# Three priorities, one planner bound and one store's queue at the end of a gated attention and state-space kernel

## The chip, the cores and the metric

The kernel runs on one core of one Trainium2 chip. The metric is the device time of one execution in microseconds (us), as the median of several runs. A profiled execution of its own gives the trace. Its span runs from the first to the last instruction, and its device time is somewhat longer than its span.

## The reference, cut to what matters

The output is a gated mix of two branches over the same sequence length of 2048 and width of 448, in bfloat16: `g * a + (1 - g) * b`, where `g` is a sigmoid per row.

```
q = (x @ wq), 16 heads of 28;  k = x @ wk;  v = x @ wv        # one key and value head for all
p = softmax(q k^T * 28 ** -0.5);   a = (p v, heads side by side) @ wo
K = Re(sum over 256 modes of C * exp(dt * A * l) * dt * B)    # 448 channels, l = 0..2047
b = causal convolution of u with K (length 2048) + u * Dskip
g = sigmoid(sum(x * gate_w));   out = g * a + (1 - g) * b
```

Both branches take the same x: the reference passes x as u.

## The kernel before, in words

The two branches are interleaved on one core.

**Attention.** There are 16 passes of 64 tiles: a pass is one group of four heads over 512 query rows, a tile is 128 keys by 512 queries. `qk` (inside `main`, L1280 and L1289) makes the scores on TensorE, ScalarE exponentiates two or three tiles at once (L1313), and `pv` (L1331) multiplies by the values and by a column of ones, which gives the softmax denominators. The last pass is walked in another order (function `dec`): queries 0 to 255, then 256 to 383, then 384 to 511, so that the first query rows are done earlier. `norm_last` then normalizes such a piece: the sums leave PSUM by a VectorE copy (`evac`, L1186), an fp32 product by a 0/1 matrix spreads the denominators over the partitions (L1201), VectorE takes the reciprocal (L1204) and multiplies (L1205).

**Output.** `outp(qc, tt)` multiplies 128 normalized rows by `Wo` in four accumulating products, g = 0 to 3 (L1155; for the very last 128 rows the same four are written out in `tail`, L1222), and `fold` (L1164) adds g times the result into the output tile `O` on VectorE. Below, "3.0" to "3.3" are the four 128-row pieces of the last 512 queries; "3.1 g3" is the fourth product of piece 3.1.

**Convolution.** For each of 28 groups of 16 channels, `conv(c)` multiplies Toeplitz blocks, which are loaded from a DRAM scratch, by the inputs (L1112), gates and flips the sum (L1127), turns it back with four small products (L1138), and adds it into `O` on VectorE (L1146). The groups 26 and 27 own the last 32 columns of `O`, which have dependence keys `Oz` of their own.

**Stores.** `tail` writes the output by DMAs. `out0` to `out3` carry the first 416 columns, four row blocks each (three for `out3`), from SyncE. `outz0` and `outz1` carry the last 32 columns in pieces of 64 bytes: `outz0` the first half of the row blocks, from GpSimd; `outz1` the rest but the last block, from ScalarE's queue. `outl0` and `outl1` carry the last row block (3.3), halves on SyncE and ScalarE. Each is one or two DMA instructions. A queue issues in order, and SyncE waits for all of them at the end.

**What sets the order.** Nothing is written by hand: `Prog.schedule` is a list scheduler that runs at build time with a planned duration for each operation. On each engine it takes, among the operations that are ready at the same planned time, the one with the lower `pr`; operations with `pr` of 2 or more also get some planned slack (`SLACK`). The result is one fixed instruction list per engine with semaphore waits. A PSUM bank is taken by the first operation with `lock` and given back by the one with `unlock`. `Prog.idle` (called for each TensorE operation) puts *zero products* into planned gaps of TensorE: products with three zero columns of `vaug`, which add nothing (L1346). It does so only while `FILL[0] < r < FILL[1]` in planned time, while the planned load of the last 3413 ns is under `LOW`, and while `self.part < 15`. That counter is set at every `pv`:

```
            t = 4 * v + 3
            pg.parts[len(pg.ops) - 1] = v % 16 if t < HF - 64 else 15
```

`HF - 64` is 896 of 1024 tiles, so from tile 896 on the counter stays at 15.

Of the kernel before, what the change touches and what calls it, by code (L numbers as in the profile page):

```python
# [66 lines left out]
def dram(t, off, dims):  # L67
    return bass.AP(tensor=t.tensor, offset=t.offset + off, ap=[list(d) for d in dims])
# [7 lines left out]
class Prog:  # L76
# [8 lines left out]
    HEAD = 0.4  # L85
    RANK = {142: -3000, 102: -1500, 107: 1500, 188: -700, 28: -1500, 23: -3000, 121: -3000, 33: 1500, 57: 1500, 93: -700, 181: -700}
    POOL = (7, 5)
    LOW, SPAN, FILL = .47, 3413.0, (36000.0, 440000.0)
    AHEAD = 1500.0
    SLACK = {"pe": 700.0, "dve": 150.0}  # L90

# [331 lines left out]
def el(n, rate=0.96, fix=68):  # L423
    return fix + n / rate
# [22 lines left out]
class Kernel:  # L447
# [647 lines left out]
    def conv(self, c):  # L1095
        pg = self.pg
        X = ("cx", c)
        cs = c % 2
        ps = px = self.grp()
        tls = []  # L1100
        for k in range(4):
            tls.append(self.tload(4 * c + k))
            if k == 0:
                ps.conv = [self.lastT, None]
                pg.convs.append(ps)
        for k in range(4):
            gi = 4 * c + k
            for n in range(8):
                def mm(e, k=k, n=n, tl=tls[k], gi=gi):
                    tbuf, to = pg.hinfo[tl.home]  # L1110
                    for j in range(4):
                        r = e.matmul(ps.v(32 * j, 32 - 2 * n, 128 * k, [[1, 128]]),  # L1112
                                     self.U.v(0, P, (4 * gi + j) * 32 + 2 * n, [[1, 32 - 2 * n]]),
                                     tbuf.v(0, P, to + j * 1024 + 896 - 128 * n, [[1, 128]]),
                                     start=(n == 0), stop=(n == 7), tile_position=(0, 32 * j), skip_group_check=True)
                    return r
                first = k == 0 and n == 0
                ps.conv[1] = len(pg.ops)
                o = pg.op("pe", mm, 56, mode="c", ni=8, rd=[("TL", gi), ("Uc", c)] + ([("U", q) for q in range(4)] if c == 0 else []),
                      wr=[X] + ([("cst", cs)] if first else []), pr=(1.6, 1.0)[c > 25],  # L1120
                      lock=ps if first else None)
                if n == 7:
                    o.tfree = tls[k]
        self.cdone[c] = o.i
        if c % 8 == 7 and c < 24:
            pg.homes.append([[self.cdone[k] for k in range(c - 7, c + 1)], NTR + c // 8])
        pg.op("dve", lambda e: e.tensor_tensor(self.cst.v(0, P, cs * 512, [[128, 4], [64, 2], [1, 64]]),  # L1127
                                               ps.v(0, P, 63, [[128, 4], [64, 2], [-1, 64]]),
                                               self.omq.v(0, P, 0, [[0, 4], [64, 2], [1, 64]]), ALU.mult),
              el(512), rd=[X, "omq"], wr=[("cst", cs), X], pr=2)  # L1130
        Y = ("yx", c)

        def yt(e, k):
            for par in range(2):
                for mu in (0, 1):
                    nt = 15 if (mu == 1 and par == 0) else 16
                    ro = 16 * (1 - par) + mu
                    r = e.matmul(px.v(64 * par, 64, 64 * k, [[16, 4], [1, nt]]),  # L1138
                                 self.cst.v(0, P, cs * 512 + 128 * k + 64 * (1 - mu), [[1, 64]]),
                                 self.ident.v(0, P, ro, [[32, 4], [1, nt]]),  # L1140
                                 start=(mu == 0), stop=(mu == 1), tile_position=(0, 64 * par), skip_group_check=True)
            return r
        for k in range(4):
            pg.op("pe", lambda e, k=k: yt(e, k), 70, mode="h", ni=8, rd=[("cst", cs), "id"], wr=[Y], pr=1.55)
        ov = self.O.v(0, P, 15 * D + 16 * c, [[-D, 16], [1, 16]])
        pg.op("dve", lambda e: e.tensor_tensor(ov, ov, px.v(0, P, 0, [[1, 16], [16, 16]]), ALU.add),  # L1146
              el(256), rd=[Y], comm=tuple(("O" if c < 26 else "Oz", q) for q in range(7)), pr=2, unlock=px)

    def outp(self, qc, tt):
        pg = self.pg  # L1150
        X = ("ox", qc, tt)
        G = self.grp()
        px = lambda: G.v(0, P, 0, [[1, D]])
        for g in range(4):
            pg.op("pe", lambda e, g=g: e.matmul(  # L1155
                px(), self.onT.v(0, P, g * 512 + 128 * tt, [[1, 128]]), self.Wo.v(0, P, g * D, [[1, D]]),
                start=(g == 0), stop=(g == 3), tile_position=(0, 0), skip_group_check=True), 200,
                rd=["Wo"] + [("on", gg) for gg in (0, 1, 2, 4 if (qc, tt) == (3, 2) else 3)], wr=[X], pr=1.2 if qc == 3 else 1.65, lock=G if g == 0 else None)
        self.fold(qc, tt, px, 0, D, [X], unlock=G)

    def fold(self, qc, tt, px, off, n, rd, unlock=None):
# [45 lines left out]
    def tail(self):  # L1207
        pg = self.pg
        self.norm_last(14, 0, 512, None, [("on", 2)])
        self.norm_last(15, 0, 256, None, [("on", 3)])  # L1210
        for tt in range(2):
            self.outp(3, tt)
        self.norm_last(15, 256, 128, None, [("on", 4)])
        self.outp(3, 2)
        self.evac(15, 384, 128)
        self.norm_last(15, 384, 128, 1, [("on", 5)])
        t, o = self.bank(2)
        px = lambda: t.v(0, P, o, [[1, D]])
        X, key = ("ox", 3, 3), [("b", 2)]
        on = [("on", 0), ("on", 1), ("on", 2), ("on", 5)]  # L1220
        for g in range(4):
            pg.op("pe", lambda e, g=g: e.matmul(  # L1222
                px(), self.onT.v(0, P, g * 512 + 384, [[1, 128]]), self.Wo.v(0, P, g * D, [[1, D]]),
                start=(g == 0), stop=(g == 3), tile_position=(0, 0), skip_group_check=True), 200,
                rd=["Wo", on[g]], wr=[X] + key, pr=1 if g < 3 else 0.5)
        self.fold(3, 3, px, 0, D, [X])
        D0 = D - 32
        n0 = len(pg.ops)
        rows = lambda t0, m, d0, n: [(dram(self.out, (1024 * h + 64 * t0) * D + d0, [[D, 64], [64 * D, m], [1, n]]),
                                      self.O.v(64 * h, 64, D * t0 + d0, [[D, m], [1, n]])) for h in range(2)]  # L1230
        for qc in range(4):
            m = 4 if qc < 3 else 3
            pg.dma(rows(4 * qc, m, 0, D0),
                   (128 * m, 832), f"out{qc}", rd=[("O", q) for q in ([qc], range(3, 6))[qc == 3]], pr=1)
        for i in range(n0, len(pg.ops)):
            pg.after[i] = self.lastT
        for k, e in enumerate(("pool", "act")):
            m = 8 - k
            pg.dma(rows(8 * k, m, D0, 32),
                   (128 * m, 64), f"outz{k}", rd=[("Oz", q) for q in (range(2), range(2, 6))[k]], pr=1, eng=e)  # L1240
        for h, e in enumerate(("sp", "act")):
            pg.dma(rows(15, 1, 0, D)[h:h + 1], (64, 896), f"outl{h}", rd=[("O", 6), ("Oz", 6)], pr=1, eng=e)
# [184 lines left out]
```

## Time and profile before

| what | value |
|---|---|
| runs of the kernel | 507.58, 508.55 and 510.98 us, median 508.55 us |
| profiled execution, device time | 510.69 us |
| its span | 508.7 us |
| mean granted TensorE clock | 0.975 of full speed |
| busy ScalarE, VectorE, TensorE | 486.1, 451.2, 433.7 us |
| last exponential ends | about 500.7 us of the span |
| last VectorE instruction ends | about 505.2 us |

How to read it: the attention's exponentials keep ScalarE busy nearly throughout. They are over at about 500.7 us, and what follows is a tail of 8 us with little work, in which the last rows are normalized, multiplied by `Wo`, added up and stored. All times below are microseconds from the start of the span. In a row of the timeline the first number is the start, the second the length, then come engine, line, operation, and the number of merged instructions; square brackets hold the idle time before it and what ended it. "SPq" and "ACTq" are the DMA-issuing instructions of SyncE's and ScalarE's queues; those of GpSimd stand under POOL.

### The profile page before, as it was taken

Reading aid. Unit: us, or ns where it says so; the run is one execution under the profiler, and the core shown is the slowest. Engines: PE = TensorE matmul, PEld = TensorE weight load, DVE = VectorE, ACT = ScalarE, POOL = GpSimd, SP = SyncE. Lnnn points to the kernel's source line nnn. Section 1 sums busy time; section 2 is a strip of 40 time slices with the busy share of each in tenths; the row PEclk is TensorE's granted clock in tenths of the full one; section 3 lists DMA queues with packets and bytes.
Section 4 is the critical chain, followed back from the end, with each engine's and each line's share of the span. In section 5 each row is a group of like instructions: output and inputs, shape, how many; then the busy total and the mean of one; then the engine's idle time right before and its main releaser. Section 6 shows DMA issues by size and latency. Waiting matters only on the chain.

```text
span 508.7 us, 18842 instructions
## 1 busy us (share of the span) xinstructions
PE 433.7 (85%) x8380; PEld 201.5 (40%) x8487; DVE 451.2 (89%) x825; ACT 486.1 (96%) x438; POOL 164.3 (32%) x304
## 2 busy tenths in 40 slices
PE   7888877887878898888888898988888898899795
PEld 5522232433424344433444443343344343443473
DVE  7999999999999999999999999999999998222264
ACT  5999999999999999999999999999999997999893
POOL 8800225412422421442251324225233325050101
PEclk9959999999999999999999999999999997999979
DMA  7988406999597996999999899997979999999902
GB/s 206 234 66 117 99 23 199 279 335 305 183 339 273 345 313 221 303 306 366 312 339 372 251 321 334 339 367 232 379 234 349 339 323 363 368 339 386 353 27 46
DMA packets 115730, 138.45 MB, mean 272 GB/s; under 512 B 48841, under 2 KB 55402, under 8 KB 115650
## 3 DMA queue, kind: packets, MB, share of 16 engines
q1 hardware_dynamic: 105872, 127.82, 79.1%
q0 software_dynamic: 8768, 9.31, 6.9%
q8 instruction: 66, 1.08, 0.9%
q10 hardware_dynamic: 1010, 0.12, 0.1%
q14 instruction: 14, 0.11, 0.1%
HBM read 125.41 MB, written 5.22 MB: 257 GB/s over the span
## 4 chain that ended last, share of the span: by engine, by line
DVE 54%; ACT 29%; PE 14%; issue 2%; DMA 1%; SPq 1%
ACT expT L1313 27%; DVE tab L1005 8%; DVE tab L1016 5%; DVE tab L1017 5%; DVE tab L1027 4%; DVE tab L1015 4%; DVE tab L1014 4%; DVE msq L948 3%; PE psS L1289 3%; DVE tmp L1023 3%; PE psB L1331 2%; PE psS L1280 2%; DVE seedz L952 2%; DVE seedz L950 2%; DVE mbf L968 2%
## 5 line engine op out<-in xcount | busy, mean ns | idle before, releaser
L1313 ACT ACTIVATE expT<-psS 128x1536 bf16<-128x1536 f32 (+1 forms) x410 | 467.1, 1326 | 8.9 <-PE psS L1280 4.7
L1289 PE MATMUL psS<-qM,kT 128*128 128x512 bf16 (+2 forms) x372 | 105.6, 360 | 29.8 <-ACT expT L1313 18.4
L1331 PE MATMUL psB<-expT,vaug 128*32 128x512 bf16 (+2 forms) x1152 | 105.2, 373 | 1.8 <-issue 0.7
L1280 PE MATMUL psS<-qT,kT 29*128 29x512 bf16 (+2 forms) x693 | 83.7, 369 | 26.9 <-ACT expT L1313 23.2
L145 POOL DMA_DIRECT2D KP_scratch<-kstg x112 | 61.4, 556 | 60.0 <-DVE kstg L1067 45.1
L1005 DVE TENSOR_TENSOR tab<-tab,mbf 128x512 bf16<-128x512 bf16 (+3 forms) x56 | 64.5, 1152 | 0.1
L1331 PEld LDWEIGHTS psB<-expT,vaug 128*32 128x32 bf16 x1152 | 28.0, 94 | 78.6 <-issue 73.4
L1289 PEld LDWEIGHTS psS<-qM,kT 128*128 128x128 bf16 x473 | 31.2, 99 | 49.5 <-ACT expT L1313 33.1
L1280 PEld LDWEIGHTS psS<-qT,kT 29*128 29x128 bf16 x693 | 21.8, 93 | 68.5 <-ACT expT L1313 52.9
L145 POOL DMA_DIRECT2D rdenB<-R_scratch x56 | 28.9, 523 | 60.7 <-DMA R_scratch<-denT 41.1
L145 POOL DMA_DIRECT2D qM<-qT x64 | 32.0, 508 | 31.4 <-DVE qT L923 16.9
L1016 DVE TENSOR_TENSOR tab<-tab 128x128 bf16<-128x128 bf16 (+4 forms) x70 | 41.7, 595 | 0.1
L1017 DVE TENSOR_TENSOR tab<-tab 128x128 bf16<-128x128 bf16 (+4 forms) x70 | 41.5, 593 | 0.0
L145 POOL DMA_DIRECT2D denT<-acc x14 | 10.6, 758 | 82.5 <-DVE acc L1186 69.1
L1112 PE MATMUL psX<-T,U 128*32 128x128 bf16 (+3 forms) x1472 | 36.6, 223 | 0.3 <-DVE O L1164 0.3
L1112 PE MATMUL psS<-T,U 128*32 128x128 bf16 (+7 forms) x1248 | 31.1, 222 | 1.5 <-issue 1.1
L1027 DVE TENSOR_TENSOR tab<-tab,tmp 128x4096 bf16<-128x4096 bf16 x14 | 31.9, 2282 | 0.1
L1014 DVE TENSOR_TENSOR tab<-tab,mbf 128x4096 bf16<-128x4096 bf16 x14 | 31.9, 2280 | 0.0
L1015 DVE TENSOR_TENSOR tab<-tab,mbf 128x4096 bf16<-128x4096 bf16 x14 | 31.9, 2280 | 0.0
L1112 PEld LDWEIGHTS psX<-T,U 128*32 128x32 bf16 (+3 forms) x1472 | 25.0, 94 | 16.7 <-issue 12.3
L1052 PE MATMUL psX<-tab 128*32 128x64 bf16 x1152 | 27.2, 242 | 1.8 <-issue 1.4
L145 POOL DMA_DIRECT2D R_scratch<-denT x14 | 8.4, 599 | 62.9 <-DVE denT L1178 35.2
(166 smaller groups left out, 551.8 us busy)
## 6 DMA issues: line engine op xcount, KB each, us to landing
T<-KP_scratch SPq DMA_DIRECT2D x170, 512.0 KB, 8.4
U<-KP_scratch SPq DMA_DIRECT2D x40, 512.0 KB, 9.6
tab<-KP_scratch SPq DMA_DIRECT2D x14, 512.0 KB, 8.2
rdenB<-R_scratch POOLq DMA_DIRECT2D x56, 64.0 KB, 5.5
qM<-qT POOLq DMA_DIRECT2D x64, 32.0 KB, 5.1
tab<-in_A_x_dram SPq DMA_DIRECT2D x8, 224.0 KB, 3.5
O<-cst SPq DMA_DIRECT2D x1, 1792.0 KB, 9.3
KP_scratch<-kstg POOLq DMA_DIRECT2D x112, 16.0 KB, 4.5
```

The lines of the kernel that those rows point to most:

```text
L145: return [e.dma_start(o, i, **kw) for o, i in pairs]
L1005: vo(lambda e, dst=dst, src=src, mri=mri: e.tensor_tensor(dst, src, mri, ALU.mult), 4 * n, done + mk(lv), [kr, ki, tk])
L1014: vo(lambda e, src=src, mi=mi, tv=tv: e.tensor_tensor(tv, src, mi, ALU.mult), 2 * n, done + mk(lv), [tk])
L1015: vo(lambda e, dst=dst, src=src, mr=mr: e.tensor_tensor(dst, src, mr, ALU.mult), 2 * n, done + mk(lv), [kr, ki, ("gap", s)])
L1016: vo(lambda e, dc=dc, tc=tc: e.tensor_tensor(dc[0], dc[0], tc[1], ALU.subtract), n, [tk, kr], [kr])
L1017: vo(lambda e, dc=dc, tc=tc: e.tensor_tensor(dc[1], dc[1], tc[0], ALU.add), n, [tk, ki], [ki])
L1027: vo(lambda e: e.tensor_tensor(tab.v(0, P, FM, [[4, 1024], [1, 4]]), tab.v(0, P, lo + 124, [[CG, 32], [-4, 32], [1, 4]]), rho.v(0, P, 0, [ ...
L1112: r = e.matmul(ps.v(32 * j, 32 - 2 * n, 128 * k, [[1, 128]]), self.U.v(0, P, (4 * gi + j) * 32 + 2 * n, [[1, 32 - 2 * n]]), tbuf.v(0, P, t ...
L1280: r = e.matmul(self.psS.v(0, P, 512 * b + o, [[1, n]]), kT.v(32 * h, DH + 1, 128 * kt, [[1, 128]]), qT.v(32 * h, DH + 1, 512 * (i % 2) + q ...
L1289: r = e.matmul(self.psS.v(0, P, 512 * b + o, [[1, n]]), kT.v(0, P, 128 * kt, [[1, 128]]), self.qM.v(0, P, (i % 2) * XQ + 512 * h + qo, [[1 ...
L1313: pg.op("act", lambda e: e.activation(expT.v(0, P, 512 * es[0], spread(es, n)), self.psS.v(0, P, 512 * bs[0], spread(bs, n)), AF.Exp, scal ...
L1331: r = e.matmul(self.psB.v(32 * h, 32, qo, [[1, n]]), vaug.v(0, P, 32 * kt, [[1, 32]]), expT.v(0, P, 512 * ring[t] + o, [[1, n]]), start=(k ...
```

## The change

Four edits in three functions and one planner constant:

- `FILL`: zero products are allowed until 490 us of planned time instead of 440 us.
- `conv`: the VectorE add of the convolution groups 26 and 27 into `O` gets `pr` 1.5 instead of 2 (and so loses the planned slack).
- `outp`: the output products of the last 512 queries get `pr` 0.9 instead of 1.2, which is below the 1 and 0.5 of `tail`'s own products in the first case and above in the second.
- `tail`: the store `outz0` is issued by SyncE instead of GpSimd.

```
-    LOW, SPAN, FILL = .47, 3413.0, (36000.0, 440000.0)
+    LOW, SPAN, FILL = .47, 3413.0, (36000.0, 490000.0)
...
-              el(256), rd=[Y], comm=tuple(("O" if c < 26 else "Oz", q) for q in range(7)), pr=2, unlock=px)
+              el(256), rd=[Y], comm=tuple(("O" if c < 26 else "Oz", q) for q in range(7)), pr=(2, 1.5)[c > 25], unlock=px)
...
-                ... wr=[X], pr=1.2 if qc == 3 else 1.65, lock=G if g == 0 else None)
+                ... wr=[X], pr=0.9 if qc == 3 else 1.65, lock=G if g == 0 else None)
...
-        for k, e in enumerate(("pool", "act")):
+        for k, e in enumerate(("sp", "act")):
             m = 8 - k
             pg.dma(rows(8 * k, m, D0, 32),
                    (128 * m, 64), f"outz{k}", rd=[("Oz", q) for q in (range(2), range(2, 6))[k]], pr=1, eng=e)
```

What the scheduler makes of it, read from the two built programs: the lists of all five engines, waits included, are the same up to the last 30 or so instructions of TensorE. The 13 zero products stand where they stood and none is added. From there the lists differ as follows (in order; each name is one instruction unless counted):

```
TensorE before  3.1 g0 g1 g2 | 3.3 g0 g1 | last pv x16 | 3.3 g2 | 3.1 g3 | 3.2 g0 | L1201 | 3.2 g1 g2 g3 | 3.3 g3
TensorE after   3.1 g0 g1 g2 g3 | 3.2 g0 | last pv x16 | 3.2 g1 g2 g3 | 3.3 g0 | L1201 | 3.3 g1 g2 | 3.3 g3
VectorE before  fold 3.0 | evac L1186 | fold 3.1 | L1204 | fold 3.2 | L1205 | fold 3.3
VectorE after   fold 3.0 | fold 3.1 | evac L1186 | fold 3.2 | L1204 | L1205 | fold 3.3
GpSimd before   ... outz0 x2                     GpSimd after   ... (ends before it)
SyncE before    out0 out1 out2 (x6) | out3 x2 | outl0
SyncE after     out0 out1 out2 (x6) | outz0 x2 | out3 x2 | outl0
```

ScalarE's list is unchanged: exponentials, then `outz1` x2, then `outl1`.

More of the change, by code (lines that the diff above doesn't have):

```diff
@@ L1157, in outp @@
                 start=(g == 0), stop=(g == 3), tile_position=(0, 0), skip_group_check=True), 200,
-                rd=["Wo"] + [("on", gg) for gg in (0, 1, 2, 4 if (qc, tt) == (3, 2) else 3)], wr=[X], pr=1.2 if qc == 3 else 1.65, lock=G if g == 0 else None)
+                rd=["Wo"] + [("on", gg) for gg in (0, 1, 2, 4 if (qc, tt) == (3, 2) else 3)], wr=[X], pr=0.9 if qc == 3 else 1.65, lock=G if g == 0 else None)
         self.fold(qc, tt, px, 0, D, [X], unlock=G)
```

## The prediction

> **What bounds the kernel now.** I read the page first (shares, the chain that ended last), then the timeline of the last 10 us engine by engine, then the DMA issues and the DMA traffic of the end.
>
> ```profile
> span 508.7 us, 18842 instructions
> PE 433.7 (85%) x8380; PEld 201.5 (40%) x8487; DVE 451.2 (89%) x825; ACT 486.1 (96%) x438; POOL 164.3 (32%) x304
> ...
> L1346 PE MATMUL psB<-vaug,ident x12: 378/390/391, 59.5 to 387.9; 128*128 128x512 bf16 x12
> ```
>
> ScalarE is busy for 486.1 of 508.7 us. But the built lists differ only in the last 30 or so instructions, so the question is what bounds the last 9 us. The chain of waits, restricted to that stretch, says it:
>
> ```profile
> 501.29 0.30 PE psS L1222
> 501.59 0.20 PE psS L1155
> ...
> 501.82 0.69 DVE O L1164
> 502.50 0.86 DVE rdenB L1204
> 503.37 0.50 DVE O L1164
> 503.87 0.21 DVE onT L1205
> ...
> 504.12 0.38 PE psS L1222
> ...
> 504.52 0.68 DVE O L1164
> ```
>
> After the last `pv` VectorE is the chain: fold 3.1, reciprocal, fold 3.2, multiplication, then one product and fold 3.3. Two folds stand in line between the last attention sums and the last product, though they do not belong to it. After that come the stores. The timeline (engines together, rows chosen) has the starts that I count with:
>
> ```profile
> 496.38 0.95 DVE L1204 RECIPROCAL rdenB<-psX 128x128 f32<-128x128 f32 x1
> ...
> 497.36 0.29 DVE L1205 TENSOR_TENSOR onT<-acc,rdenB 128x128 bf16<-128x128 f32 x1
> ...
> 497.75 0.42 DVE L1146 TENSOR_TENSOR O<-O,psS 128x256 bf16<-128x256 bf16 x1
> ...
> 498.46 1.44 POOL L145 DMA_DIRECT2D out_dram<-O  x2 [24.33 <-DVE O L1146]
> ...
> 500.41 0.54 PE L1222 MATMUL psS<-Wo,onT 128*128 128x448 bf16 x2
> ...
> 500.88 0.41 PE L1331 MATMUL psB<-expT,vaug 128*32 128x128 bf16 x16
> ...
> 501.23 0.36 PE L1222 MATMUL psS<-Wo,onT 128*128 128x448 bf16 x1
> ...
> 501.35 0.29 DVE L1186 COPY acc<-psB 128x128 f32<-128x128 f32 x1 [1.28 <-PE psB L1331]
> 501.42 0.54 PE L1155 MATMUL psS<-Wo,onT 128*128 128x448 bf16 x2
> ...
> 501.80 0.38 PE L1201 MATMUL psS<-acc,msq 128*128 128x128 f32 x2
> ...
> 502.42 0.95 DVE L1204 RECIPROCAL rdenB<-psS 128x128 f32<-128x128 f32 x1
> 503.28 0.59 DVE L1164 SCALAR_TENSOR_TENSOR O<-psS,gt,O 128x448 bf16<-128x448 f32 x1
> 503.78 0.28 DVE L1205 TENSOR_TENSOR onT<-acc,rdenB 128x128 bf16<-128x128 f32 x1
> ```
>
> From these rows: products of 448 columns start 0.19 apart (501.23, 501.42). A fold starts 0.40 after the start of its last product (501.42 to 501.82; 504.12 to 504.52) and lets the next VectorE instruction start 0.60 later (501.82 to 502.42). A multiplication starts 0.34 before the product that uses it (503.78 to 504.12).
>
> **The change part by part.**
>
> *Zero products until 490.* Costs and gains nothing. The row of L1346 has the last one at 387.9, so the old bound of 440 was not what stopped them: from tile 896 of 1024 the counter `part` is 15 and forbids them. The built list has the same 13 in the same places (12 of them have a record in the trace). Would they come, each would cost about 0.39 of TensorE.
>
> *The convolution add's priority.* Nothing by itself: both adds keep their place in VectorE's list. The last is at 497.75, ahead of fold 3.0, in both.
>
> *`outz0` from SyncE.* GpSimd loses two issues (1.44 in all, at 498.46), and nothing stands behind them there. SyncE gains a wait for the add that ends at 498.17 and two issues. Queued behind that wait are `out3` and `outl0`. The queue rows of the end, one narrow window each:
>
> ```profile
> 503.90 0.72 ACTq L145 DMA_DIRECT2D out_dram<-O  x1
> 503.90 1.99 SPq L145 DMA_DIRECT2D out_dram<-O  x3
> 505.23 0.65 SPq L145 DMA_DIRECT2D out_dram<-O  x1
> 505.51 0.95 ACTq L145 DMA_DIRECT2D out_dram<-O  x1
> ```
>
> SyncE issues nothing between its first six stores and 503.90. A pair of 64-byte stores takes ScalarE's queue from 503.90 to 505.51, 1.61. On SyncE the pair would run from 498.2 to 499.8, and `out3` will not be wanted before 502.7 (below): hidden by 2.9, cost 0. Its landing:
>
> ```profile
> T<-KP_scratch SPq DMA_DIRECT2D x1, 512.0 KB, 13.6
> out_dram<-O SPq DMA_DIRECT2D x2, 156.0 KB, 2.8
> ...
> out_dram<-O POOLq DMA_DIRECT2D x2, 32.0 KB, 2.2
> out_dram<-O ACTq DMA_DIRECT2D x2, 28.0 KB, 3.2
> out_dram<-O SPq DMA_DIRECT2D x1, 56.0 KB, 2.8
> out_dram<-O ACTq DMA_DIRECT2D x1, 56.0 KB, 2.7
> ```
>
> Bounds are 2.2 (the same store from GpSimd) and 13.6 (a load on SyncE's queue amid full traffic). I take 3.2, the same 64-byte shape on ScalarE's queue: the second lands at about 499.0 + 3.2 = 502.2, long before the end. At 13.6 it would land at 512.6 and set the end; that is a rival.
>
> *The output products' priority.* This is the edit that moves something. TensorE, in the new order, with the pace of 0.19 and the last `pv` left at 500.88 (it waits for ScalarE, and five products stand ahead of it as before):
>
> - 3.1 g3 takes the place at 500.41, and 3.2 g0 that at 500.60. Fold 3.1 starts at 500.81 instead of 501.82, when VectorE is idle, and frees it at 501.41.
> - The copy L1186 now stands behind fold 3.1: 501.41 instead of 501.35, a cost of 0.06. What waits for the copy is L1201.
> - After `pv`: 3.2 g1, g2, g3 at 501.23, 501.42, 501.61, 3.3 g0 at 501.80, L1201 at 501.99 instead of 501.80, because four products stand ahead of it instead of three. Its operand is ready at about 501.75. Done at 502.37.
> - Fold 3.2 starts at 501.61 + 0.40 = 502.01, ends at 502.70, frees VectorE at 502.61. Before it started at 503.28, after the reciprocal.
> - The reciprocal starts at 502.61 instead of 502.42, a loss of 0.19. But no fold follows it. The earlier 128-column reciprocal started 0.98 before its multiplication (496.38 to 497.36). So L1205 starts at 503.59 instead of 503.78, the last product at 503.93, fold 3.3 at 504.33, and its end comes at 505.01 instead of 505.20: 0.19 gained.
> - The stores. `out3` and `outz1` wait for fold 3.2 and can go at 502.73 instead of 503.90, 1.17 earlier. That matters on ScalarE's queue: before, `outl1` was ready at 505.2 but stood behind the pair of `outz1` until 505.51. Now the pair is through at 502.73 + 1.61 = 504.34, so `outl1` goes with the data, at 505.04, 0.47 earlier. `outl0` goes at 505.04 instead of 505.23.
>
> *The last landing.* Before: 505.51 + 2.7 = 508.2 for `outl1`, 505.23 + 2.8 = 508.0 for `outl0`; the span ends 0.5 after the later. With unchanged landings the later is now `outl0` at 507.84: 0.37 gained. The other end: both last stores share the DMA engines with `out3` and `outz1`, which now start 1.17 earlier. The windows of the end show that all traffic is one block of 2.4:
>
> ```profile
> 502.00:505.00 3.00, 1.12 (x6) 0.31 (x4) 2.54 (x5) 0.00 (x0) 0.00 (x0) 1.00 0.00 0
> 505.00:508.70 3.70, 0.00 (x0) 0.00 (x0) 0.21 (x1) 0.00 (x0) 0.00 (x0) 0.76 0.58 133
> ...
> 506.90:507.50 0.60, 0.00 (x0) 0.00 (x0) 0.00 (x0) 0.00 (x0) 0.00 (x0) 0.52 0.99 218
> 507.50:508.10 0.60, 0.00 (x0) 0.00 (x0) 0.00 (x0) 0.00 (x0) 0.00 (x0) 0.50 0.09 28
> ```
>
> (The last two columns are the DMA share and GB/s.) If the block splits, the last stores may land like the only output store of the end that ran alone, GpSimd's 2.2: 507.24, a gain of 0.97. I take the middle, 0.65, since the other stores still overlap part of the last ones. Below nothing the landing has no reason to go, as less is in flight.
>
> [...]
>
> *Sum.* 508.7 - 0.65 = 508.05 of span. The profiled execution took 510.69, 1.99 more than its span, so it would take 510.04. But it is a slow one, 2.14 above the median of the runs (508.55); the median should come to 508.55 - 0.65 = 507.9.
>
> **The rivals.**
>
> - *Nothing gained: the tail is hidden.* If the last landing is set by the whole block of traffic or by a completion that does not depend on its issue, the end stays: 508.5. For it: the DMA share is 0.99 just before the end. Against it: the block's first half starts 1.17 earlier, and 504.0 to 505.1 was free.
> - *Slower: the reciprocal is pushed back.* In the new list two folds stand ahead of the reciprocal. Gain and loss balance where fold 3.2 starts at 502.20 instead of 502.01, since the reciprocal would then start at 502.80 and the multiplication at the old 503.78. If each of the four products takes 0.1 more than I count, or 3.1 g3 does not get out before the last `pv` (then fold 3.1 starts at 501.23 + 0.40, frees VectorE at 502.23, and all behind it is 0.82 behind my list), the last fold ends at up to 505.83 instead of 505.20. `outl0` then goes at 505.86 and lands at 508.66 instead of `outl1` at 508.21: 0.45 slower, a median of 509.0.
> - *Slower: SyncE's small store lands late.* Mechanism: 64-byte pieces on SyncE's ring, landing after the last store. It decides from a landing of about 8.6 (the forecast's last landing at 508.2 - 0.65 = 507.55, less 499.0), and at the bound of 13.6 the last landing is at 512.6 instead of 508.2, 4.4 later: a median of 512.95. Against it: 3.2 on ScalarE's queue, and a DMA share of 0.13 from 498 to 502:
>
> ```profile
> 498.00:502.00 4.00, 4.00 (x77) 2.18 (x76) 1.32 (x4) 2.70 (x3) 1.44 (x2) 1.00 0.13 18
> ```
>
> - *The change does not do what it says.* True for the first edit, as said, and for the second. If the moved products bring nothing either, this is the first rival.
>
> **How the numbers follow.** Forecast (gain 0.37 to 1.04): 0.75. Nothing gained: 0.12. Reciprocal pushed back: 0.11. Late landing: 0.02. The likeliest gives 507.9. The forecast's own bounds are 507.5 to 508.2; the pushed-back case adds 509.0. The runs before lie 0.97 below and 2.43 above their median, and that spread is wider than any term here, so I take about 0.5 beyond the cases at either side: 506.9 to 509.5. One per cent, 5.1 us, is about what a measurement of this kernel can tell from no change, and every case but an extreme landing stays far inside it: within 1% 0.97, faster 0.01, slower 0.02.
>
> **What would show it right or wrong.** Right: fold 3.1 at about 500.8 and ahead of the copy; fold 3.2 about 0.4 to 0.6 before the reciprocal; no fold between reciprocal and multiplication; `out3` and `outz1` issued about 1.2 earlier; `outl1` issued with `outl0`; no traffic left over at their issue; 13 zero products, the last near 388; the pair of `outz0` on SyncE near 498.2. Wrong: a copy later than 501.6, a reciprocal later than 502.8, `outl1` still behind `outz1`, or an `outz0` landing near the end. A difference of more than 2 us anywhere before 499 would mean that something moved which the lists do not show.

## The result and the profile after

The changed kernel takes 507.46 us in the median (505.21 to 509.80, 20 runs); the kernel before, run beside it, 509.27 us (507.19 to 511.44, 20 runs). The ratio is 0.9964, with a 95% interval from 0.9947 to 0.9981. That is 1.8 us less, or 1.0 to 2.7 us by the interval: the same within 1%, as forecast, and faster by more than the 0.65 us forecast.

The profiled execution after took 507.12 us with a span of 505.1 us, against 508.7 before. Most of these 3.6 us are not the change. The last `pv` group started at 500.88 before and starts at 498.32 now, and up to a few products ahead of it the instruction lists are the same, but for the small store that SyncE now issues; below, two executions of one and the same list differ by 4.8 us. So I measure the tail, from the start of the last `pv` group to the end of the span. The rows of that stretch (start, end and length, the busy times of the engines, and last the granted clock, the DMA share and GB/s), before and after:

```profile
500.88:508.69 7.81, 2.24 (x26) 1.06 (x25) 3.22 (x6) 0.00 (x0) 0.00 (x0) 0.89 0.28 63
```

```profile
498.32:505.14 6.82, 2.24 (x26) 1.14 (x25) 3.33 (x6) 0.00 (x0) 0.00 (x0) 0.84 0.33 72
```

The tail takes 7.81 before and 6.82 after: the change is worth 0.99 there. (The expectations below count with spans printed to 0.1, and so with 7.82 and 6.78.) The four edits are two priorities, one bound and one queue; the title counts one priority too many.

The timeline of the changed kernel's tail, the rows that answer to those of the prediction:

```profile
497.27 1.12 PE L1155 MATMUL psS<-Wo,onT 128*128 128x448 bf16 x5
498.24 0.69 DVE L1164 SCALAR_TENSOR_TENSOR O<-psS,gt,O 128x448 bf16<-128x448 f32 x1 [0.74 <-PE psS L1155]
...
498.32 0.41 PE L1331 MATMUL psB<-expT,vaug 128*32 128x128 bf16 x16
...
498.84 0.28 DVE L1186 COPY acc<-psB 128x128 f32<-128x128 f32 x1
...
499.43 0.38 PE L1201 MATMUL psS<-acc,msq 128*128 128x128 f32 x2
499.44 0.68 DVE L1164 SCALAR_TENSOR_TENSOR O<-psS,gt,O 128x448 bf16<-128x448 f32 x1 [0.32 <-PE psS L1155]
...
500.04 0.95 DVE L1204 RECIPROCAL rdenB<-psS 128x128 f32<-128x128 f32 x1
...
501.03 0.29 DVE L1205 TENSOR_TENSOR onT<-acc,rdenB 128x128 bf16<-128x128 f32 x1
...
501.37 0.36 PE L1222 MATMUL psS<-Wo,onT 128*128 128x448 bf16 x1 [1.18 <-DVE onT L1205]
501.78 0.68 DVE L1164 SCALAR_TENSOR_TENSOR O<-psS,gt,O 128x448 bf16<-128x448 f32 x1 [0.46 <-PE psS L1222]
```

What to see: fold 3.1 (498.24) now starts ahead of the last `pv` group, in VectorE's old gap; fold 3.2 (499.44) stands ahead of the reciprocal, and between reciprocal (500.04) and multiplication (501.03) there is no fold. Counted from the last `pv` group, fold 3.3 ends at 4.14 instead of 4.32.

The queues of the changed kernel, one narrow window each, and then its DMA issues with the KB of each and the us to landing:

```profile
495.63 1.27 SPq L145 DMA_DIRECT2D out_dram<-O  x2
...
500.16 2.85 ACTq L145 DMA_DIRECT2D out_dram<-O  x3
...
502.49 0.50 SPq L145 DMA_DIRECT2D out_dram<-O  x1
502.49 0.52 ACTq L145 DMA_DIRECT2D out_dram<-O  x1
```

```profile
out_dram<-O SPq DMA_DIRECT2D x2, 156.0 KB, 2.7
...
out_dram<-O SPq DMA_DIRECT2D x2, 32.0 KB, 2.6
out_dram<-O ACTq DMA_DIRECT2D x2, 28.0 KB, 3.1
out_dram<-O SPq DMA_DIRECT2D x1, 56.0 KB, 1.9
out_dram<-O ACTq DMA_DIRECT2D x1, 56.0 KB, 2.2
```

`outz1` starts at 500.16, 2.33 ahead of the last stores (before, 1.33 ahead of `outl0` and 1.61 ahead of `outl1`), and `outl0` and `outl1` go together at 502.49, with their data. They land in 1.9 and 2.2 instead of 2.8 and 2.7. The 0.99 is made up of 0.18 (end of fold 3.3), 0.28 (`outl1` no longer behind `outz1`: it was issued at 505.51 where `outl0` went at 505.23), and some 0.5 (landing of `outl1`, 2.7 to 2.2, which are known to 0.1).

Why they land earlier is in the DMA engines' busy share. Each digit is that share in tenths (9 is 90% or more) in a slice of 0.12 us; both rows end with the span. Before (from 503.88), then after (from 500.32):

```profile
DMA  0000000000289999874459999889995000000000
```

```profile
DMA  0000000006989988744799999902697930000000
```

Before, the traffic is one block up to 507.6: the last stores' data come right behind those of `out3` and `outz1`. After, the others are still at work when the last stores are issued at 502.49, but they are through at about 503.5; then there is a gap, and the last stores' data follow alone.

### The profile page after: what moved, and what is told of

Same layout as the page of the kernel before. It is cut to its first block, busy times and chain, and to the rows that moved or that the text cites. A ratio compares the mean times of both kernels' runs of the same rounds, so it can differ in the third digit from the quotient of the medians.

```text
span 505.1 us, 18842 instructions
## 1 busy us (share of the span) xinstructions
PE 432.4 (86%) x8380; PEld 200.1 (40%) x8487; DVE 451.7 (89%) x825; ACT 486.3 (96%) x438; POOL 162.9 (32%) x302
## 4 chain that ended last, share of the span: by engine, by line
ACT 44%; DVE 35%; PE 16%; issue 3%; DMA 1%; SPq 1%
ACT expT L1313 43%; DVE tab L1005 5%; PE psS L1289 3%; DVE tab L1016 3%; DVE tab L1017 3%; PE psB L1331 3%; PE psS L1280 3%; DVE tab L1027 3%; DVE tab L1015 3%; DVE tab L1014 3%; DVE msq L948 2%; PE psS L1112 2%; DVE tmp L1023 2%; DVE seedz L952 1%; DVE mbf L968 1%
```

## The experiments

Each ratio is to the kernel before, run beside it on the same chip. The medians themselves are from several chips (the kernel before had 508.41 beside e1 to e4, 508.12 beside e5 to e8 and 509.39 beside e9 to e12), so only the ratios can be compared. "Tail" is the time from the start of the last `pv` group to the end of the span in that kernel's one profile; where the number of runs is 1, the profiled execution is all there is.

| kernel | median us (runs) | ratio to before, 95% interval | last pv, span | tail us |
|---|---|---|---|---|
| before | 509.27 (20) | 1 | 500.88, 508.69 | 7.81 |
| changed | 507.46 (20) | 0.9964, 0.9947 to 0.9981 | 498.32, 505.14 | 6.82 |
| e1 order only | 506.82 (12) | 0.9965, 0.9941 to 0.9988 | 497.31, 504.15 | 6.84 |
| e2 store only | 507.62 (12) | 0.9972, 0.9947 to 0.9997 | 498.99, 506.81 | 7.82 |
| e3 same lists as before | 508.90 (12) | 1.0005, 0.9982 to 1.0027 | 496.35, 504.16 | 7.81 |
| e4 changed, again | 507.20 (12) | 0.9974, 0.9950 to 0.9999 | 500.01, 506.83 | 6.82 |
| e5 before, outz1 from GpSimd | 518.1 (1) | | 503.16, 515.92 | 12.77 |
| e6 changed, early stores delayed | 508.16 (12) | 0.9994, 0.9971 to 1.0016 | 497.47, 504.29 | 6.82 |
| e7 changed, fold 3.2 behind | 506.35 (1) | | 496.44, 504.28 | 7.84 |
| e8 before, early stores delayed | 509.94 (12) | 1.0027, 0.9998 to 1.0055 | 500.14, 508.03 | 7.89 |
| e9 order only, GpSimd's store later | 513.42 (1) | | 502.68, 511.42 | 8.74 |
| e10 changed, out3 with full rows | 508.02 (12) | 0.9972, 0.9952 to 0.9991 | 497.13, 503.96 | 6.83 |
| e11 store only, again | 507.96 (12) | 0.9988, 0.9965 to 1.0011 | 498.05, 505.88 | 7.83 |
| e12 same lists, again | 510.05 (12) | 1.0025, 1.0001 to 1.0049 | 501.17, 509.03 | 7.86 |

The theories: A, the new order of the output products is all of the gain, and it lies in the tail; B, the store's move to SyncE gains too. C and D (a stall near 479) and E (GpSimd's closing drain) came up on the way.

**e1: the order alone.** Of the four edits only this one:

```
-                ... wr=[X], pr=1.2 if qc == 3 else 1.65, ...
+                ... wr=[X], pr=0.9 if qc == 3 else 1.65, ...
```

> Only the output products' priority (0.9), the store stays on GpSimd. Theory A (the order of the tail is all of it): from the start of the last pv group to the end of the span 6.8 us as in the changed kernel (7.82 before, 6.78 after), fold 3.2 about 0.6 before the reciprocal, outl1 issued with outl0; time about 1.0 us under the kernel before. Theory B (the store's move to SyncE brings the rest of the 1.8): the tail is at most 0.3 shorter than before, or the time is 0.8 us longer than that of the changed kernel.

Measured: a tail of 6.84 and a ratio of 0.9965. Fold 3.2 starts 0.60 ahead of the reciprocal, and `outl1` is issued with `outl0`, as expected. For the tail theory A holds to within 0.02. The time fell by 1.8, where A expected 1.0.

**e2 and e11: the store alone.**

```
-        for k, e in enumerate(("pool", "act")):
+        for k, e in enumerate(("sp", "act")):
```

> Only outz0 from SyncE instead of GpSimd, order of the products as before. Theory A: tail from the last pv group to the end 7.8 us, time equal to the kernel before within 0.7 us; the pair is issued when the last convolution add is done and lands within 3.5 us. Theory B: the time falls by about 0.8 us.

> outz0 from SyncE alone, once more. Theory A (no effect but through the closing drain, which the old order hides): time of the kernel before within 0.7 us, tail 7.8. Rival (something ahead of the tail gets faster): 1.4 us under the kernel before again, as the first time.

Measured: tails of 7.82 and 7.83, so nothing in the tail. The times were 0.9972 the first time, outside of what theory A allowed, and 0.9988 the second, inside it. The traces show no place where such a gain would arise.

**e3 and e12: the two edits that change no list.**

```
-    LOW, SPAN, FILL = .47, 3413.0, (36000.0, 440000.0)
+    LOW, SPAN, FILL = .47, 3413.0, (36000.0, 490000.0)
...
-              ... for q in range(7)), pr=2, unlock=px)
+              ... for q in range(7)), pr=(2, 1.5)[c > 25], unlock=px)
```

> Only the later bound for zero products and the convolution add's priority: the built instruction lists are those of the kernel before. Theory A: ratio 1.000, tail 7.8 us, 13 zero products, the last near 388; what the medians of this run differ by from the kernel before is the size of the scatter. Rival (the scatter is a property of the build): a ratio clearly off 1, by 0.8 us or more.

> The instruction lists of the kernel before, once more, as the yardstick for the store-only kernel on the same chip: ratio 1.000 within 0.0015, tail 7.8.

Measured: tails of 7.81 and 7.86, and the zero products where they were, the last at 388.7 in e12:

```profile
L1346 PE MATMUL psB<-vaug,ident x13: 379/389/390, 59.6 to 388.7; 128*128 128x512 bf16 x13
```

The times are what matters here: with the instruction lists of the kernel before, the ratio came out at 1.0005 and at 1.0025, the second outside the 0.0015 expected and with an interval that leaves 1 out. So a ratio of this kernel is uncertain by some 0.0025, 1.3 us, more than its own interval says. The spans of the two profiles differ by 4.8 us.

**e4: the changed kernel once more.** No edit.

> The changed kernel once more. Theory A: tail 6.8 us again, and a time about 1.0 us under the kernel before, so 0.998 of it, nearer to that than to the 0.9964 measured. Rival (something before the tail became faster too): 0.9964 again, 1.8 us, with the start of the last pv group earlier than in the kernels with the old order.

Measured: tail 6.82, ratio 0.9974. The tail repeats to 0.01 where the ratio moves by 0.0010, 0.5 us. The interval holds both the 0.998 of theory A and the 0.9964 of its rival, so the time does not decide. Nor does the last `pv` group start earlier with the new order: between 497.13 and 500.01 in the changed kernel, e1, e4 and e10, between 496.35 and 501.17 in the kernel before, e2, e3, e11 and e12.

**e5: free ScalarE's queue, leave the order.** On the kernel before:

```
-        for k, e in enumerate(("pool", "act")):
+        for k, e in enumerate(("pool", "pool")):
```

> The kernel before, with outz1 issued by GpSimd (behind outz0), so that outl1 has ScalarE's queue to itself; products and folds in the old order, out3 at its old time. Theory A (the stores' gain of 0.86 us after fold 3.3 has two parts, the queue and the earlier traffic): outl1 is issued with outl0 at the end of fold 3.3, 0.28 earlier, but both still land 2.6 to 2.8 later, since out3 and outz1 are in flight as before; tail from the last pv group to the end 7.6 to 7.8 us. Rival (the queue alone is the gain): landing 2.2 or less, tail 7.0.

Measured: a tail of 12.77, which no theory had. `outl1` was indeed issued with `outl0` (both at 507.51), and both landed later than ever, in 3.3 and 3.2: with the pieces of `outz1` in flight at that time, only from another queue, the free queue alone brings no early landing. But the end came 5 us after the landing. The closing instructions of each engine (line of the block's end; number, lengths in ns, first and last start) show why:

```profile
L471 POOLq EVENT_SEMAPHORE  x2: 17/17/17, 515.7 to 515.8; - x2
...
L471 POOLq DRAIN  x1: 8840/8840/8840, 506.9 to 506.9; - x1
...
L471 SPq DRAIN  x1: 13/13/13, 511.1 to 511.1; - x1
```

The last stores had landed by 510.8 (507.51 + 3.3), and SyncE's drain started at 511.1. GpSimd's closing drain, started at 506.9 between its last two issues, took 8.84 and ended at 515.7; the last semaphore instructions of the other engines start at 515.9, and the span ended at 515.92.

**e7: put fold 3.2 back behind the reciprocal.** On the changed kernel, extra planned slack for that fold:

```
-                        t += self.SLACK.get(x.eng, 0.0)
+                        t += self.SLACK.get(x.eng, 0.0) + 600.0 * (x.pr == 2.5)
...
-        ... ("Oz", qc + tt * (qc == 3))), pr=2, unlock=unlock)
+        ... ("Oz", qc + tt * (qc == 3))), pr=2.5 if (qc, tt) == (3, 2) else 2, unlock=unlock)
```

> The changed kernel, but fold 3.2 stands behind the reciprocal again, as before the change; TensorE's list as in the changed kernel. Theory A: the reciprocal starts about 0.2 earlier than in the changed kernel, the multiplication about 0.2 later, fold 3.3 ends 0.2 later, and out3 and outz1 are issued 1.1 later, so outl1 again waits for outz1 (0.3 behind fold 3.3): tail 7.4 to 7.7. Rival (fold 3.1's early place is what gains): tail 6.8 to 7.0.

Measured: the tail is 7.84, that of the kernel before, and a little above the 7.4 to 7.7 expected, since the landings went back all the way to 2.8 and 2.7. Its VectorE timeline and last stores:

```profile
497.97 0.96 DVE L1204 RECIPROCAL rdenB<-psS 128x128 f32<-128x128 f32 x1 [0.73 <-PE psS L1201]
498.84 0.58 DVE L1164 SCALAR_TENSOR_TENSOR O<-psS,gt,O 128x448 bf16<-128x448 f32 x1
499.34 0.28 DVE L1205 TENSOR_TENSOR onT<-acc,rdenB 128x128 bf16<-128x128 f32 x1
```

```profile
out_dram<-O SPq DMA_DIRECT2D x1, 56.0 KB, 2.8
out_dram<-O ACTq DMA_DIRECT2D x1, 56.0 KB, 2.7
```

With TensorE's new list kept, one fold's place gives back the whole gain. Fold 3.1's early place alone brings nothing: the reciprocal starts 1.53 after the last `pv` group, and 1.54 before, now held by L1201, which stands behind one more product.

**e6 and e8: delay the early stores.** All profiles show TensorE idle for 1.5 to 2.0 near 479 with no releaser, and all but that of e10 then at half clock; in the kernel before, 1.25 MB of stores (6 x 208 KB, issued from 472.2 to 478.7, landing in 7.3 to 10.6) are in flight there. On the changed kernel and on the one before, the first of them now waits for a later VectorE copy instead of what it waited for (the copy is at 487.4 in the profile before; `ev` is its number):

```
-                    for s, v in o.waits.items():
+                    for s, v in ({"dve": ops[self.ev].count[1]} if o.slot == "out0" else o.waits).items():
```

> The changed kernel, same instruction lists, but the first of the early stores (out0 to out2, 6 x 208 KB) waits for VectorE's copy at about 487, so the 1.25 MB is not in flight when TensorE waits at 479 for nothing that the profile shows. Theory C (that wait is TensorE's own instruction load, slowed by the stores; the half clock after it follows from the idle time): the idle time of 1.5 to 2.0 us shrinks below 0.8, the half-clock stretch after it shrinks or goes, the last pv group starts before 498, and the time falls by 1.5 to 4 us against the changed kernel; the tail stays 6.8. Rival D (the loads ahead of the stores slow it, or the wait has another cause): idle time and half clock as before, time unchanged within 0.8 us.

> The kernel before with the same delay of the early stores. Theory C: the same fall as between the changed kernel and its delayed form, 1.5 to 4 us against the kernel before; tail 7.8. Rival D: no difference beyond 0.8 us.

Measured: theory C fell. The stall is as long as before, in e6:

```profile
477.83 0.28 PE L1280 MATMUL psS<-qT,kT 29*128 29x256 bf16 x3 [1.74 <-issue]
```

The first store was issued at 484.2 there, so the stores do not cause the stall. Other traffic stayed, though: during the stall of e6 (476.1 to 477.8) the DMA engines moved 373 to 389 GB/s in windows of 0.5 us, all ahead of SyncE's first store. And in the kernel before and in the changed one, a 16 KB packet of instructions is in flight as the stall begins (478.8 to 479.9, with a stall from 479.6; 476.7 to 477.8, with a stall from 477.6), while such packets come every 5.0 to 7.1 us around it and the neighbouring ones bring no stall. An instruction load that is slowed by this other traffic is therefore possible, and not shown. Neither kernel became faster: 0.9994 where the changed kernel has 0.9964, and 1.0027 where the kernel before has 1. Both lean to slower by about as much as e12, which changes nothing, so no more is read from that. What the stall waits for stays open.

**e9: dose the drain.** On the order-only kernel, `outz0` stays on GpSimd and waits for fold 3.0 too:

```
-  ... rd=[("Oz", q) for q in (range(2), range(2, 6))[k]], pr=1, eng=e)
+  ... rd=[("Oz", q) for q in (range(2), range(2, 6))[k]] + [("O", 3)] * (1 - k), pr=1, eng=e)
```

> The order-only kernel with outz0 still from GpSimd, but waiting for fold 3.0 as well, so that GpSimd's last issue comes about 1.6 later against the last pv group. Theory E (GpSimd's closing drain, 8.6 us long and starting at its last DMA issue, is at the end of the order-only kernel as long as the stores themselves, and hidden by 1.0 in the kernel before): tail from the last pv group to the end 6.9 + 1.6 = 8.5 us, SyncE's closing instructions done 1.5 before the end. Rival (the drain ends when the other engines do, and costs nothing): tail 6.9.

Measured: a tail of 8.74, against 8.5 expected and 6.84 without the delay. Counted from the last `pv` group, GpSimd's pair is issued 1.9 later than in e1, where 1.6 was expected, and the tail is longer by the same 1.9. The pair goes at 502.15, and its closing instructions run on for 2 us after SyncE's:

```profile
L471 POOLq EVENT_SEMAPHORE  x2: 17/17/17, 511.2 to 511.3; - x2
L471 POOLq DRAIN  x1: 8572/8572/8572, 502.6 to 502.6; - x1
...
L471 SPq DRAIN  x1: 13/13/13, 509.3 to 509.3; - x1
```

The same drain in the kernel before, and in the order-only kernel (e1):

```profile
L471 POOLq DRAIN  x1: 8567/8567/8567, 498.9 to 498.9; - x1
...
L471 SPq DRAIN  x1: 12/12/12, 508.5 to 508.5; - x1
```

```profile
L471 POOLq DRAIN  x1: 8573/8573/8573, 495.3 to 495.3; - x1
...
L471 SPq DRAIN  x1: 13/13/13, 503.9 to 503.9; - x1
```

It is 8.57 long in all three. Before, it ended at 498.9 + 8.57 = 507.5, 1.0 ahead of SyncE's 508.5. In e1 it ends at 495.3 + 8.57 = 503.9, with SyncE's. Theory E holds: the new order used up the cover that GpSimd's store had. In the changed kernel the drain starts at 471.4 and is far out of the way.

**e10: no small pieces after fold 3.2.** On the changed kernel, `out3` takes all 448 columns, `outz1` only the four row blocks before, sent after the last copy:

```
-            pg.dma(rows(4 * qc, m, 0, D0),
+            pg.dma(rows(4 * qc, m, 0, (D0, D)[qc == 3]),
...
-            m = 8 - k
+            m = 8 - 4 * k
```

(with the dependences that go with it)

> The changed kernel, but out3 carries all 448 columns of its three row blocks, and outz1 only the four row blocks before them, which it can send right after the last pv group's copy. After fold 3.2 no 64-byte pieces are left to send. If the traffic of outz1 still delays the last landing (2.2 for outl1, 1.9 for outl0), the tail falls from 6.8 to 6.4 to 6.6 us; if 2.2 is the floor of such a store, it stays 6.8. Time 1.0 to 1.4 us under the kernel before.

Measured: tail 6.83 and the same landings:

```profile
out_dram<-O SPq DMA_DIRECT2D x1, 56.0 KB, 1.9
out_dram<-O ACTq DMA_DIRECT2D x1, 56.0 KB, 2.2
```

So taking the pieces of `outz1` out of the way brings nothing beyond 2.2, and this version gains nothing on the changed kernel.

## Why the prediction was right, and where it fell short

- *Bound and mechanism: right.* VectorE's chain after the last `pv` group and the stores behind it set the end; e7 shows that fold 3.2's place ahead of the reciprocal is the gain (a tail of 7.84 without it, 6.82 with it).
- *The chain's terms: right.* Counted from the last `pv` group, the prediction had fold 3.1 at -0.07 (measured -0.08), the copy at 0.53 (0.52), fold 3.2 at 1.13 (1.12), the reciprocal at 1.73 (1.72), the multiplication at 2.71 (2.71), the end of fold 3.3 at 4.13 (4.14). `outl1` was to go 0.47 earlier and went 0.46 earlier.
- *The last landing: too small.* The step "I take the middle, 0.65" failed. Between 2.7 and 2.2 the prediction chose halfway because some of the other stores' traffic would still overlap. At the issue it did overlap, so its sign "no traffic left over at their issue" did not come. But the last stores' data began only about 1.1 after their issue, when the others were through (the gap in the DMA row above), and nothing was left of the delay: 2.2 for `outl1` in the changed kernel, e1, e4, e6, e9 and e10, 2.7 or 2.8 in every kernel whose fold 3.2 came behind the reciprocal, except e5 with 3.2. Which of the two stores' traffic causes the delay the runs do not separate; e10 only shows that `outz1` is not needed for the 2.2. The tail's gain is 0.99; the prediction's other end, worked out with the lone store's 2.2, was 0.97. No run shows the 1.04 at the far end of the forecast's gain, nor the 507.5 that follows from it: the two last stores landed in 1.9 and 2.2, and the tail gained 0.99.
- *`outz0` from SyncE at no cost: right as a change of its own, but a cover was not named.* The pair landed in 2.6, where the prediction took 3.2, far from the end. The prediction looked for what stands behind the two issues on GpSimd and found nothing. The closing drain of 8.57 stood there, hidden by 1.0 before, and with the new order by nothing. The move is worth 0.02 at most here (6.84 against 6.82), but had the order gained more, the store would have had to move first.
- *Zero products and the convolution add: right.* No list changed, and the tails of e3 and e12 are those of the kernel before.
- *The median: 1.8 less where the tail explains 0.99.* The tail's gain lies at the near end of the interval (0.97 to 2.7). The four kernels with the new order and the early stores in their old place measured 0.9964, 0.9965, 0.9974 and 0.9972; those with the same early lists and the old order 1.0005, 1.0025, 0.9972 and 0.9988. The means of the two groups lie 0.0029 apart, 1.5 us, and the spread within them is 0.0010 and 0.0053. Scatter of this size covers the rest. So the tail's gain was predicted for the right reason; that the median moved by 1.8 is in part luck. That something ahead of the tail also became faster is not excluded and not shown.

## What to carry to other kernels

Where one engine in order holds both the chain to the end and work that only happens to be there, try to move that work ahead of the chain's wait. Here it paid twice: the chain lost it (0.18), and what hung on it (two stores) started 1.2 earlier and was out of the way of the last transfer (0.28 and some 0.5). Before trusting a store that "nothing stands behind", look at the closing instructions of its engine as well: here a drain of 8.57 was hidden by 1.0 in the kernel before, and with the new order (e1) by nothing, since both it and SyncE's ended at 503.9. And when a change sits in a short stretch, measure that stretch from a common event: here the tail repeats within 0.1 us, the whole kernel only within several us.

## What the runs showed of the hardware that was not expected

GpSimd's closing drain starts between the two issues of its last pair of stores (at 498.9 in the kernel before, with the issues at 498.5 and 499.2) and takes 8.57 us (8,567 to 8,573 ns in before, e1, e3, e8, e9 and e12), although each of these 32 KB stores lands in 2.1 to 2.4. After two pairs it takes 8.84 (e5). When its last DMAs are the four loads near 471, it takes 9.5 to 9.7 and is hidden (in the changed kernel it ends at 480.9, 24 us ahead of the end). SyncE's drain takes 12 or 13 ns. What the drain waits for the traces do not say.

The stall near 479 is followed, in every profile but that of e10, by a stretch at half clock (in e9 it begins within the stall, at 481.7), and the lengths of these stretches are one, two or three times the same step. Mean granted clock from 474 to 496 (third column from the right) in e10, e3, the changed kernel and e8, in this order:

```profile
474.00:496.00 22.00, 18.02 (x536) 12.14 (x528) 10.71 (x14) 20.58 (x19) 0.00 (x0) 1.00 0.47 147
```

```profile
474.00:496.00 22.00, 19.46 (x504) 12.86 (x493) 11.03 (x14) 20.78 (x19) 1.44 (x2) 0.92 0.49 153
```

```profile
474.00:496.00 22.00, 19.98 (x506) 13.02 (x503) 10.35 (x13) 20.35 (x18) 0.00 (x0) 0.84 0.47 148
```

```profile
474.00:496.00 22.00, 19.60 (x477) 13.19 (x466) 9.06 (x11) 18.83 (x17) 0.00 (x0) 0.77 0.51 151
```

The windows of 0.5 us that lie wholly inside the stretch have a clock of 0.50, those wholly outside 1.00. Twice the missing share of 22 us gives 0, 3.5, 7.0 and 10.1 us; summed over these windows it is 0, 3.41, 6.83 and 10.23. All 14 profiles have one of these four, to 0.01. From the start of the last product ahead of the stall to the last `pv` group they take 20.4 us with no step, 20.2 to 20.9 with one, 20.9 to 21.7 with two, and 22.3 to 22.7 with three, so this is one source of the scatter, worth up to 2.5 us (22.7 less 20.2); that start itself, 475.8 to 482.0, is a larger one. The stall's idle time does not go with the number of steps: 1.47 is followed by none in e10 and by two in the changed kernel, 2.02 by one in e1 and by three in e9. And a busy TensorE was at half clock too: in e8 it was busy for 9.74 of the 10 us from 480.5 to 490.5, all at 0.50. What sets the number of steps the traces do not show.
